# Another table of due-time shifts in a list-scheduled attention and MLP kernel on one core

## The chip, the core and the metric

The kernel runs on one core of a Trainium2 chip. The core has a matrix engine (TensorE, PE, with its weight loads PEld), a vector engine (VectorE, DVE), a scalar engine (ScalarE, ACT), a general engine (GpSimd, POOL) and a queue engine (SyncE, SP) that issues nearly all transfers. The metric is device time in microseconds for one execution; less is better. Instructions of one engine run in the order in which the program issued them; engines wait for one another through semaphores. So an order that is planned ahead is the order that the chip must follow.

## What is computed

Four batches of four heads, 1088 tokens, head size 32. Each token is projected twice to eight numbers (S1 and S2); the outer product of both is its feature vector of 64. Linear attention is made of these features, and its result, 4352 tokens of 128, goes through a two-layer MLP with a leaky relu whose slope is given per hidden unit.

```
def phi(x):
    a = np.einsum('rd,bhsd->bhsr', S1, x)
    b = np.einsum('rd,bhsd->bhsr', S2, x)
    return np.einsum('bhsi,bhsj->bhsij', a, b).reshape(*x.shape[:-1], r * r)
q_p, k_p = (phi(q), phi(k))
kv = np.einsum('bhsf,bhsd->bhfd', k_p, v)
z = np.sum(k_p, axis=2)
num = np.einsum('bhsf,bhfd->bhsd', q_p, kv)
den = np.einsum('bhsf,bhf->bhs', q_p, z)[..., None] + 1e-06
...
h = x @ w_in
g = np.maximum(h, 0.0) + alpha * np.minimum(h, 0.0)
return (g @ w_out)
```

## The kernel before

The kernel is written as a list of 762 operations, each with an engine (or several to choose from), a duration for each, what it depends on and which buffers it holds. A planner (`plan`, from line 168) puts them in order at build time, and the kernel then emits them in that order.

**What the operations are.** For each batch b, the keys side makes features in two halves: `kb.0T` and `kb.1T` transpose, `...ab` projects (L636), `...abc` copies out of PSUM, `...kp` multiplies (L653). Batch 0 transposes on PE (L626), the others on DVE (L681). The last 64 tokens of each batch are the rest: `kr0.0`, `kr0.1` and `kr1`. `z0.0`, `z0.1`, `zr0` (L719, L733) and `kv0.0`, `kv0.1`, `kvr0` (L706, L726) accumulate the sums over tokens. `zm`, `finz`, `zc` (L751, L757, L763 and 764) bring the sum z into the form that the denominator needs; `kvc`, `fin`, `kvW` (L361, L766, L361) do this for the numerator.

The queries side: `qT` transposes on DVE (L855 for batch 0, which is cut into the halves `q0.0` and `q0.1`; L815 otherwise), `a` and `b` project on PE (L872 or L828), `ac0`, `ac1` copy and `mul0`, `mul1` multiply (L884 or L842). Then `ratio`: `den` and `num` on PE (L785), `dT` transposes the denominator (L792), `rc` takes the reciprocal (L798, L799), `rr` spreads it by a transpose (L801), and `x0`, `x1` multiply it with the numerator (L807). `x0` of `q0.0` is what the first MLP matmul waits for.

The MLP works in ten chunks g of tokens: seven of 512 and three of 256. Each has 16 matmuls `hg.c` (L955), each with a relu `rg.c` on ACT (L961) or DVE (L963), 16 matmuls `og.c` (L976; L973 in the last chunk) that add to one PSUM bank, and one more, `Wg`, with the product W of both weights, for the leaky part. `oTg` transposes the sum (L983) and `stg` stores it by SP. All o-matmuls of all chunks but the last share PSUM bank 7, so `o1.0` can't start before `oT0` has read it. Eight buffers hold relu results and at most four PSUM banks hold h.

The weights are prepared on the way, in four parts each: `w_in_bf` casts w_in (ACT or DVE, L361), `w_a` scales w_out for the o-matmuls (ACT at L573, or DVE or POOL at L556), `w_b` scales it for W (ACT or POOL), `w_hi` and `w_lo` split w_b in two bf16 parts, `winT` and `winTc` transpose w_in, `Wmm` (L598) and `W` (L604, L605) make W.

**What sets the order.** The planner takes due times from the MLP, which is given 10.2 us per chunk of 512 from 14.5 us on, and passes them backward: an operation is due 1.6 times the duration (plus latency and 70 ns) ahead of the earliest that needs it. To each due time it adds the entry of a table `SHIFT`, in ns. Then it steps through the list: among the first 120 operations still waiting by due time, those whose inputs are planned are candidates; on each engine the one that is due first wins among those that can start within 120 to 300 ns of the earliest, and over the engines the one that starts first is placed. An operation that may go to two engines is put where it ends first. Where PE would idle between 4 and 20 us, fill matmuls (L499) are put in. So the table changes order and, for operations with a choice, the engine, and also the number of fills; instructions and data stay as they are. Loads have names that begin with `ld` and due times near -1,000,000; no entry of the table names one.

```
for o in ops:
    o.due += SHIFT.get(o.name, 0)
waiting = sorted(ops, key=lambda o: o.due)
```

Inherited due times (before the shift), in ns, of the operations that matter later: kr0.0T 1,370; q0.0b 3,342; zr0 3,661; zm0 4,317; kvr0 8,021; kvc0 8,693; q0.0rc 9,179; fin0 9,239; q0.1T 11,556; w_in_bf 12,147 (first part); w_b0 to w_b3 15,763; w_a1 15,873; w_lo0 to w_lo3 17,873; w_a3 20,783; W0 23,445.

Of the kernel before, what the change touches and what calls it, by code (L numbers as in the profile page):

```python
# [34 lines left out]
class Op:  # L35
# [30 lines left out]
    "S": 6140, "W": -7785, "W0": 1995, "W1": -3593, "W2": 5, "W3": -3870, "W4": -6766, "W5": 16353,  # L66
    "W6": -376, "W7": 10186, "W8": -1052, "W9": -1646, "Wmm": -6987, "alpha": -2765, "alphaT": -56356,
    "fin0": 14889, "fin1": -96, "fin2": 6846, "fin3": 4117, "finz0": 414, "finz1": -2297, "finz2": 14064,
    "finz3": 14913, "h0.0": -48890, "h0.1": -44482, "h0.10": -20550, "h0.11": -20506, "h0.12": -20265,
    "h0.13": -19045, "h0.14": -18399, "h0.15": -12121, "h0.2": -42632, "h0.3": -37456, "h0.4": -25806,  # L70
    "h0.5": -22156, "h0.6": -21957, "h0.7": -22369, "h0.8": -22128, "h0.9": -21948, "h1.0": -6078,
    "h1.1": -6568, "h1.10": -4424, "h1.11": -3438, "h1.12": -3826, "h1.13": -2710, "h1.14": -896,
    "h1.15": -1170, "h1.2": -5552, "h1.3": -4703, "h1.4": -4984, "h1.5": -3823, "h1.6": -4399, "h1.7": -4190,
    "h1.8": -3910, "h1.9": -4410, "h2.0": -635, "h2.1": 32, "h2.10": 137, "h2.11": -311, "h2.12": -365,
    "h2.13": -528, "h2.14": -850, "h2.15": -1064, "h2.2": -533, "h2.3": -1016, "h2.4": -1486, "h2.5": -1619,
    "h2.6": -824, "h2.7": -937, "h2.8": -591, "h2.9": -530, "h3.0": -2018, "h3.1": -920, "h3.10": -705,
    "h3.11": -966, "h3.12": -493, "h3.13": -526, "h3.15": 55, "h3.2": -1159, "h3.3": -730, "h3.4": -1309,
    "h3.5": -1793, "h3.6": -2054, "h3.7": -2660, "h3.8": -2424, "h3.9": -1487, "h4.0": -1546, "h4.1": -2165,
    "h4.10": -2919, "h4.11": 400, "h4.13": 89, "h4.14": -69, "h4.15": -83, "h4.2": -876, "h4.3": -488,
    "h4.4": -976, "h4.5": -1517, "h4.6": -2066, "h4.7": -2461, "h4.8": -2353, "h4.9": -2894, "h5.0": -1154,  # L80
    "h5.1": -1149, "h5.10": -295, "h5.11": -640, "h5.12": -1074, "h5.13": -1192, "h5.14": 291, "h5.15": 217,
    "h5.2": -1589, "h5.3": -1771, "h5.4": -1691, "h5.5": -1874, "h5.6": -1510, "h5.7": -1214, "h5.8": 88,
    "h5.9": -205, "h6.0": -207, "h6.1": 288, "h6.10": -1799, "h6.11": -2260, "h6.12": -2137, "h6.13": -1884,
    "h6.14": -207, "h6.15": -104, "h6.2": -207, "h6.3": -360, "h6.4": -101, "h6.5": -327, "h6.6": -529,
    "h6.7": -810, "h6.8": -1438, "h6.9": -2068, "h7.0": -975, "h7.1": -920, "h7.10": -1394, "h7.11": -993,
    "h7.12": -885, "h7.13": -667, "h7.14": 74, "h7.15": 22, "h7.2": -1209, "h7.3": -1250, "h7.4": -1497,
    "h7.5": -1686, "h7.6": -1144, "h7.7": -1096, "h7.8": -1336, "h7.9": -1256, "h9.0": -56, "h9.1": 634,
    "h9.10": 1533, "h9.11": 1394, "h9.12": 3304, "h9.13": 4471, "h9.14": 8625, "h9.15": 30374, "h9.2": 1277,
    "h9.3": 1488, "h9.4": 1818, "h9.5": 2075, "h9.6": 1949, "h9.7": 1698, "h9.8": 1822, "h9.9": 1642,
    "ident": -5301, "identb": 4245, "k0.0T": -338245, "k0.0Tc": -222654, "k0.0ab": -204581,  # L90
    "k0.0abc": -148771, "k0.0kp0": -2818, "k0.0kp1": -2947, "k0.1T": -290955, "k0.1Tc": -106980,
    "k0.1ab": -55631, "k0.1abc": -158, "k0.1kp0": -2312, "k0.1kp1": -1676, "k1.0T": -7361, "k1.0ab": -5266,
    "k1.0abc": -4605, "k1.0kp": 499, "k1.1T": -6359, "k1.1ab": -6458, "k1.1abc": -5045, "k1.1kp": -4738,
    "k2.0T": -28437, "k2.0ab": -4092, "k2.0abc": -1298, "k2.0kp": 2242, "k2.1T": 2146, "k2.1ab": 2146,
    "k2.1abc": 5610, "k2.1kp": 6306, "k3.0T": -25545, "k3.0ab": -24652, "k3.0abc": -23865, "k3.0kp": 1001,
    "k3.1T": 149, "k3.1ab": -1456, "k3.1abc": 580, "k3.1kp": 1938, "kr0.0T": -46499, "kr0.0Tc": -14777,
    "kr0.0ab": -12941, "kr0.0abc": -1149, "kr0.1T": -4092, "kr0.1Tc": -3579, "kr0.1ab": -3528,
    "kr0.1abc": -3313, "kr1T": -16436, "kr1Tc": -9432, "kr1ab": -1384, "kr1abc": 9835, "kv0.0": -2625,
    "kv0.1": 1851, "kv1": -996, "kv2": 4392, "kv3": 818, "kvW1": -5462, "kvW2": 7589, "kvW3": 17434,
    "kvc0": 5255, "kvc1": 78, "kvc2": 7320, "kvr0": 2609, "kvr1": 2446, "kvr2": 8823, "kvr3": 11490,  # L100
    "mask4": -1518, "masks": -28026, "o0.0": -12138, "o0.1": -1771, "o0.10": -3699, "o0.11": 89, "o0.12": 42,
    "o0.13": 5930, "o0.14": 98, "o0.15": -3161, "o0.2": -320, "o0.3": -3922, "o0.4": -4360, "o0.5": -3046,
    "o0.6": -82, "o0.7": -13490, "o0.8": -7352, "o0.9": -5660, "o1.0": -53, "o1.1": 8059, "o1.10": 14816,
    "o1.11": 22404, "o1.12": 449, "o1.13": 4844, "o1.14": 17486, "o1.15": 7036, "o1.2": 6355, "o1.3": -71,
    "o1.4": -32, "o1.5": 8264, "o1.6": 11885, "o1.7": 9436, "o1.8": 21020, "o1.9": 15581, "o2.0": 3602,
    "o2.1": 25261, "o2.10": 14347, "o2.11": 6322, "o2.12": 174, "o2.13": -321, "o2.14": 1774, "o2.15": 2276,
    "o2.2": 21551, "o2.3": 10241, "o2.4": 13814, "o2.5": 21013, "o2.6": -90, "o2.7": 11854, "o2.8": 108,
    "o2.9": 935, "o3.0": 2349, "o3.1": 20927, "o3.10": 8081, "o3.11": 5347, "o3.12": 608, "o3.13": 11675,
    "o3.14": 1466, "o3.2": 8241, "o3.3": 12758, "o3.4": 22143, "o3.5": 5685, "o3.6": 3532, "o3.7": 481,
    "o3.8": 4495, "o3.9": 23059, "o4.1": 497, "o4.10": 8949, "o4.11": 8, "o4.13": 4363, "o4.14": -225,  # L110
    "o4.15": 121, "o4.2": 1775, "o4.3": 2282, "o4.4": 1603, "o4.5": -1726, "o4.6": -78, "o4.7": 24007,
    "o4.8": 617, "o4.9": 1000, "o5.0": 4551, "o5.1": 22714, "o5.10": 18207, "o5.11": -425, "o5.12": 2511,
    "o5.13": -144, "o5.14": 9197, "o5.15": 5612, "o5.2": 13081, "o5.3": 15045, "o5.4": 17002, "o5.5": 2911,
    "o5.6": 10540, "o5.7": 8104, "o5.8": -342, "o5.9": -144, "o6.0": -25, "o6.1": 6809, "o6.10": 2075,
    "o6.11": 1537, "o6.12": 19356, "o6.13": -1218, "o6.14": 223, "o6.15": 16936, "o6.2": 15551, "o6.3": 1979,
    "o6.4": 986, "o6.5": 2904, "o6.6": 11826, "o6.7": 20308, "o6.8": 7660, "o6.9": 8842, "o7.0": 260,
    "o7.1": 211, "o7.10": 29630, "o7.11": 4680, "o7.12": 10219, "o7.13": 711, "o7.14": 25929, "o7.15": 27443,
    "o7.2": 2632, "o7.3": 268, "o7.4": 5360, "o7.5": -423, "o7.6": 19131, "o7.7": 14612, "o7.8": 3,
    "o7.9": 52263, "o8.0": 1783, "o8.1": 22008, "o8.10": 27673, "o8.11": 23944, "o8.12": 4252,
    "o8.13": 126570, "o8.14": 37728, "o8.15": 3387, "o8.2": 3039, "o8.3": 51554, "o8.4": 16336, "o8.5": 6119,  # L120
    "o8.6": 379, "o8.7": 18531, "o8.8": 42466, "o8.9": 1979, "o9.0": 2274, "o9.1": 10388, "o9.10": 49229,
    "o9.11": 22575, "o9.12": 56832, "o9.13": 49904, "o9.14": 30415, "o9.15": 66470, "o9.2": 61690,
    "o9.3": 52093, "o9.4": 17752, "o9.5": 24707, "o9.6": 38495, "o9.7": 76119, "o9.8": 27064, "o9.9": 46410,
    "oT0": -12790, "oT1": -408, "oT2": -3211, "oT3": 4518, "oT4": 616, "oT5": -3024, "oT6": -7579,
    "oT7": -1161, "oT8": -2287, "oT9.0": -536, "oT9.1": -449, "q0.0T": -219038, "q0.0a": -202701,
# [942 lines left out]
```

## Time and profile before

| | us |
|---|---|
| median of 5 runs | 113.79 |
| lowest and highest of them | 111.95, 114.03 |
| profiled execution, its own time | 112.38 |
| its span, first to last instruction | 110.6 |
| PE busy in it | 105.3 |
| DVE busy | 83.2 |
| ACT busy | 75.9 |
| POOL busy | 24.1 |

The profile is of one execution. A row of the timeline gives start, duration, engine, source line, operation, output and inputs with shapes, the count, and in brackets how long the engine had idled before and what released it. In the chain of waits each piece is what the next had to wait for, followed back from the end; "issue" is time in which nothing visible was waited for. Matmuls overlap: one of 512 columns is listed with 0.38 us, but the next starts 0.215 us after it, so PE's busy time says that work was there, not how dense it was. The granted clock is given in tenths of full speed.

### The profile page before, as it was taken

To read this page: it belongs to the slowest core of one execution; us is meant where nothing else is said; L and a number is where in the kernel's file an instruction comes from. 1 tells how busy PE (TensorE), PEld (TensorE's weight loads), DVE (VectorE), ACT (ScalarE), POOL (GpSimd) and SP (SyncE) were. 2 spreads that over 40 slices of the span, in tenths; PEclk is the share of its full clock that TensorE was granted. 3 is DMA by queue.
4 is the path that set the end of the run, shared out by engine and by line. 5 is a ranking of instruction groups with operands and counts; after the bars stand their busy time and mean duration, and the time that the engine had idled before them with its cause. 6 is when DMAs were issued, how large, how long until landed. Compare 5 with 4: busy or idle time off the path is not lost.

```text
span 110.6 us, 3534 instructions
## 1 busy us (share of the span) xinstructions
PE 105.3 (95%) x1458; PEld 54.5 (49%) x1458; DVE 83.2 (75%) x156; ACT 75.9 (69%) x162; POOL 24.1 (22%) x24
## 2 busy tenths in 40 slices
PE   7999988989999999999999999999999999999980
PEld 2577333534454663447443353444534544588870
DVE  3188869898998488996667978986548798669840
ACT  2454599998489681891983963597596278787880
POOL 2040089990029108921500000000000000000000
PEclk9999999999999999999999999999999999999999
DMA  2999999779589640041002200050040005033222
GB/s 59 264 300 286 306 277 335 134 247 297 79 272 280 99 79 0 6 71 30 0 0 47 48 6 0 6 92 3 0 81 14 6 0 95 0 56 57 33 49 59
DMA packets 37536, 11.25 MB, mean 102 GB/s; under 512 B 27008, under 2 KB 37520, under 8 KB 37520
## 3 DMA queue, kind: packets, MB, share of 16 engines
q1 hardware_dynamic: 37264, 10.95, 42.9%
q8 instruction: 11, 0.18, 0.7%
q10 hardware_dynamic: 256, 0.08, 0.3%
q14 instruction: 5, 0.04, 0.1%
HBM read 8.80 MB, written 2.23 MB: 100 GB/s over the span
## 4 chain that ended last, share of the span: by engine, by line
PE 75%; DMA 8%; SPq 7%; POOL 5%; issue 2%; ACT 0%; DVE 0%; DVEq 0%
PE ps L976 26%; PE ps L955 24%; DMA w_out_f<-in_moe_w_out_dram 8%; SPq L385 7%; PE ps L785 7%; PE ps L828 6%; PE ps L636 3%; PE ps L706 3%; POOL w_b_f L556 2%; POOL w_a_bf L556 2%; PE ps L973 2%; PE ps L598 2%; POOL w_hl L556 1%; PE ps L757 1%; PE ps L726 1%
## 5 line engine op out<-in xcount | busy, mean ns | idle before, releaser
L955 PEld LDWEIGHTS <-w_in_bf 128*128 128x128 bf16 x160 | 15.0, 97 | 15.4 <-issue 3.6
L955 PE MATMUL ps<-xT__96,w_in_bf 128*128 128x512 bf16 (+1 forms) x80 | 21.5, 358 | 0.4 <-ACT rh__82 L961 0.4
L976 PEld LDWEIGHTS <-w_a_bf 128*128 128x128 bf16 x144 | 13.6, 97 | 14.4 <-issue 2.0
L955 PE MATMUL ps<-xT__97,w_in_bf 128*128 128x512 bf16 (+1 forms) x80 | 19.2, 336 | 0.0
L961 ACT ACTIVATE rh__82<-ps 128x512 bf16<-128x512 f32 (+1 forms) x23 | 12.6, 548 | 4.9 <-PE ps L955 4.6
L961 ACT ACTIVATE rh__83<-ps 128x512 bf16<-128x512 f32 (+1 forms) x22 | 11.9, 542 | 3.6 <-PE ps L955 3.6
L961 ACT ACTIVATE rh__84<-ps 128x512 bf16<-128x512 f32 (+1 forms) x16 | 8.5, 531 | 0.9 <-PE ps L955 0.6
L961 ACT ACTIVATE rh__86<-ps 128x512 bf16<-128x512 f32 (+1 forms) x14 | 7.9, 562 | 1.0 <-PE ps L976 0.5
L792 DVE STREAM_TRANSPOSE dt__78<-ps 128x1024 f32<-128x1024 f32 (+2 forms) x6 | 5.6, 937 | 3.6 <-PE ps L785 3.6
L976 PE MATMUL ps<-rh__83,w_a_bf 128*128 128x512 bf16 (+1 forms) x22 | 7.9, 359 | 0.0
L961 ACT ACTIVATE rh__87<-ps 128x512 bf16<-128x512 f32 (+1 forms) x12 | 6.2, 518 | 2.0 <-PE ps L955 1.8
L961 ACT ACTIVATE rh__85<-ps 128x512 bf16<-128x512 f32 x11 | 6.6, 604 | 0.9 <-PE ps L955 0.9
L976 PE MATMUL ps<-rh__82,w_a_bf 128*128 128x512 bf16 (+1 forms) x20 | 7.3, 363 | 0.0
L976 PE MATMUL ps<-rh__84,w_a_bf 128*128 128x512 bf16 (+1 forms) x19 | 6.8, 357 | 0.3 <-POOL w_a_bf L556 0.3
L976 PE MATMUL ps<-rh__86,w_a_bf 128*128 128x512 bf16 (+1 forms) x20 | 7.1, 353 | 0.0
L976 PE MATMUL ps<-rh__85,w_a_bf 128*128 128x512 bf16 (+1 forms) x19 | 6.8, 356 | 0.0
L828 PE MATMUL ps<-qT__74,Sab 32*64 32x512 f32 x96 | 6.7, 613 | 0.0
L983 DVE STREAM_TRANSPOSE oT__91<-ps 128x512 f32<-128x512 f32 (+1 forms) x8 | 5.4, 680 | 1.6 <-PE ps L976 1.5
L963 DVE TENSOR_SCALAR rh__85<-ps 128x256 bf16<-128x256 f32 (+1 forms) x10 | 5.3, 527 | 1.7 <-PE ps L955 1.0
L963 DVE TENSOR_SCALAR rh__86<-ps 128x512 bf16<-128x512 f32 (+1 forms) x8 | 4.4, 552 | 2.5 <-PE ps L955 1.0
L976 PE MATMUL ps<-rh__87,w_a_bf 128*128 128x512 bf16 (+1 forms) x17 | 6.0, 355 | 0.0
L653 POOL TENSOR_TENSOR kp__70<-ab__68 128x1024 f32<-128x1024 f32 x2 | 3.9, 1956 | 9.5 <-ACT ab__68 L361 4.8
(157 smaller groups left out, 216.4 us busy)
## 6 DMA issues: line engine op xcount, KB each, us to landing
out_dram<-oT__91 SPq DMA_DIRECT2D x28, 64.0 KB, 1.9
k<-in_k_dram SPq DMA_DIRECT2D x3, 512.0 KB, 4.1
q<-in_q_dram SPq DMA_DIRECT2D x3, 512.0 KB
v<-in_v_dram SPq DMA_DIRECT2D x12, 128.0 KB, 5.4
w_in_f<-in_moe_w_in_dram SPq DMA_DIRECT2D x2, 512.0 KB, 7.0
w_out_f<-in_moe_w_out_dram SPq DMA_DIRECT2D x2, 512.0 KB, 7.9
k<-in_k_dram SPq DMA_DIRECT2D x2, 256.0 KB, 3.2
q<-in_q_dram SPq DMA_DIRECT2D x2, 256.0 KB
```

The source lines that it names most:

```text
L385: (nc.sync if eng == "sp" else nc.scalar).dma_start(dst, src)
L556: return lambda e: (nc.vector if e == "dve" else nc.gpsimd).tensor_tensor(out=out, in0=a, in1=b, op=what)
L636: nc.tensor.matmul(ps(bf)[lo + i:lo + i + aw, j * 64:(j + 1) * 64], sb(bT)[:, j * cnt + i:j * cnt + i + aw], S12blk.rearrange("p h c -> p ...
L653: (nc.vector if e == "dve" else nc.gpsimd).tensor_tensor(out=dst, in0=i0, in1=i1, op=ALU.mult)
L785: nc.tensor.matmul(dst, w, mv, start=True, stop=True, skip_group_check=True)
L792: nc.vector.transpose(bview(sb(dt), [[1, nn]]).rearrange("p (c n) -> p c n", c=2), ps(bd)[:, :, :ncp])
L828: nc.tensor.matmul(ps(bufs[t // 2])[64 * c:64 * c + 64, t % 2, :nf], bview(Sab[32 * t:32 * t + 32, i], [[1, R]]), moving(sb(bq), t, c), st ...
L955: nc.tensor.matmul(ps(b)[:, :n], w_in_bf[:, c * 128:(c + 1) * 128], xs(), start=True, stop=True)
L961: nc.scalar.activation(sb(br)[:, :n], ps(b)[:, :n], ACTF.Relu)
L963: nc.vector.tensor_scalar_max(sb(br)[:, :n], ps(b)[:, :n], 0.0)
L976: nc.tensor.matmul(ps(bo)[:, :n], w, y(), start=c == 0, stop=c == NC)
L983: o = op("dve", dv(n) + 40, lambda e: nc.vector.transpose(bview(sb(boT), [[1, n]]), ps(bo)[:, :n]), [last], [bo, boT], 80, end, f"oT{g}")
```

## The change

The whole change is another table `SHIFT`, with 699 entries in place of 675. All else, `plan` among it, is the same. The diff, cut to entries that the text below speaks of and some of their neighbours:

```
 SHIFT = {
...
-    "S": 6140, "W": -7785, "W0": 1995, "W1": -3593, "W2": 5, "W3": -3870, "W4": -6766, "W5": 16353,
+    "S": -7836, "Sab": -21631, "W": -9717, "W0": 13130, "W1": -2261, "W2": 158, "W3": -5573, "W4": -762,
...
-    "fin0": 14889, "fin1": -96, "fin2": 6846, "fin3": 4117, "finz0": 414, "finz1": -2297, "finz2": 14064,
+    "alphaT": -113674, "fin0": -197, "fin1": 1558, "fin2": 5231, "fin3": 10679, "finz0": -6860, "finz1": 259,
...
-    "k3.1T": 149, "k3.1ab": -1456, "k3.1abc": 580, "k3.1kp": 1938, "kr0.0T": -46499, "kr0.0Tc": -14777,
+    "k3.1abc": 1165, "k3.1kp": 1931, "kr0.0T": -61323, "kr0.0Tc": -47226, "kr0.0ab": -29513, "kr0.0abc": 2222,
...
-    "kv0.1": 1851, "kv1": -996, "kv2": 4392, "kv3": 818, "kvW1": -5462, "kvW2": 7589, "kvW3": 17434,
-    "kvc0": 5255, "kvc1": 78, "kvc2": 7320, "kvr0": 2609, "kvr1": 2446, "kvr2": 8823, "kvr3": 11490,
+    "kvW3": 13555, "kvc0": -17087, "kvc2": 1986, "kvc3": 1108, "kvr0": -12312, "kvr1": 2269, "kvr2": 7638,
...
-    "q0.0ac0": -192252, "q0.0ac1": 14918, "q0.0b": -4711, "q0.0dT": -153737, "q0.0den": -156593,
-    "q0.0mul1": -3827, "q0.0num": -101573, "q0.0rc": 1638, "q0.0rr": -126171, "q0.0x0": -47987, "q0.1T": 1102,
+    "q0.0T": -240062, "q0.0a": -215260, "q0.0ac0": -192157,
+    "q0.0ac1": -8807, "q0.0b": 685, "q0.0dT": -181547, "q0.0den": -190132, "q0.0mul0": -3079,
+    "q0.0mul1": 10478, "q0.0num": -89181, "q0.0rc": -14012, "q0.0rr": -163676, "q0.0x0": -80815,
+    "q0.1T": 2090,
...
-    "w_a1": 933, "w_a2": 9447, "w_a3": -1769, "w_b0": -3090, "w_b1": 20475, "w_b2": -17819, "w_b3": -1940,
+    "st9.1": 68233, "w_a0": 3313, "w_a1": 10350, "w_a2": 10033, "w_a3": 9313, "w_b0": -5006, "w_b1": 539,
+    "w_b2": -7570, "w_b3": -9465,
...
-    "w_in_bf": 1696, "w_lo0": 3902,
+    "w_in_bf": 4483,
+    "w_lo0": 15386,
...
-    "zm0": -9912,
+    "zm0": -44722, "zr0": -22838,
 }
```

zr0 has no entry before. The lines of the diff are cut here to the entries in question, so some are shorter than in the source.

## Prediction

> **What bounds the kernel now.** I read the page first, then the chain of waits in order of time, then busy time by windows, then the timeline. The page says what is full:
>
> ```profile
> PE 105.3 (95%) x1458; PEld 54.5 (49%) x1458; DVE 83.2 (75%) x156; ACT 75.9 (69%) x162; POOL 24.1 (22%) x24
> PEclk9999999999999999999999999999999999999999
> PE 75%; DMA 8%; SPq 7%; POOL 5%; issue 2%; ACT 0%; DVE 0%; DVEq 0%
> ```
>
> PE is busy for 95% of the span at full granted clock, and three quarters of the chain are PE. The chain in order of time says when it is something else:
>
> ```profile
> 9.00 8.43 DMA w_out_f<-in_moe_w_out_dram
> ...
> 17.50 2.04 POOL w_b_f L556 x2
> ...
> 22.78 1.01 POOL w_a_bf L556
> ...
> 23.83 0.82 PE ps L976 x3
> ...
> 51.17 0.30 DVE fs__99 L751
> 51.49 0.28 ACT fs__100 L361
> ```
>
> Until 23.83 the end hangs on the second half of w_out and on POOL's preparation of it. From there to 107.5 the chain is PE but for one gap of about 0.6 us at 51. Then 3.1 us of last copy and store follow. Busy time by windows (length, then PE, PEld, DVE, ACT and POOL with their instructions, clock, DMA) shows which engines are full while the pipeline fills:
>
> ```profile
> 12.00:16.00 4.00, 3.71 (x62) 1.46 (x55) 2.63 (x6) 2.65 (x8) 1.79 (x2) 1.00 1.11 275
> 16.00:20.00 4.00, 3.58 (x29) 1.26 (x28) 3.68 (x6) 3.97 (x8) 3.86 (x5) 1.00 1.16 322
> 20.00:24.00 4.00, 3.66 (x29) 1.99 (x28) 3.99 (x6) 4.00 (x9) 4.00 (x5) 1.00 0.63 154
> ```
>
> Between 16 and 24 ACT, DVE and POOL are full and PE is not; between 12 and 16 ACT and DVE idle a third of the time, because h0.0 has not started. The timeline shows the chain of the first reciprocal, and two lines that I need later:
>
> ```profile
> 6.98 1.12 PE L872 MATMUL ps<-qT__74,Sab 32*64 32x256 f32 x32
> 8.03 0.27 PE L626 MATMUL ps<-ident,kr 64*128 64x64 f32 x1
> 8.62 0.22 ACT L361 COPY kT__64<-ps 128x64 f32<-128x64 f32 x1
> 8.76 1.30 DVE L884 TENSOR_TENSOR aq__76<-ps,aq__76 128x512 f32<-128x512 f32 x2
> 11.37 0.70 DVE L855 STREAM_TRANSPOSE qT__74<-q 128x512 f32<-128x512 f32 x1
> 11.52 0.66 PE L785 MATMUL ps<-aq__76,zc 64*32 64x256 f32 x16
> 12.29 0.72 DVE L792 STREAM_TRANSPOSE dt__78<-ps 128x512 f32<-128x512 f32 x1 [0.21 <-PE ps L785]
> 14.84 0.69 DVE L807 TENSOR_TENSOR xT__96<-ps,rr__80 128x512 bf16<-128x512 f32 x1 [0.58 <-PE ps L785]
> ...
> 22.73 1.05 POOL L556 TENSOR_TENSOR w_a_bf<-w_out_f,omaT 128x512 bf16<-128x512 f32 x1
> ...
> 33.06 0.38 PE L976 MATMUL ps<-xT__96,W_bf 128*128 128x512 bf16 x1
> ```
>
> The denominator (L785) starts at 11.52 though its products (L884) end at 10.06: it waits for z, which waits for the k rest (8.03, 8.62). x0 (L807) then idles 0.58 us for the numerator.
>
> **The change, part by part.** The table alone changes, so work per engine is the same, but for operations that may go to one of two engines. A due time is the inherited one, which the backward pass of the source gives, plus the shift, in the planner's ns. I compare these sums, old to new, and do not know the order that comes of them.
>
> *First chain.* The k-rest transpose falls from -45,129 to -59,953, zr0 from 3,661 to -19,177, zm0 from -5,595 to -40,405, and the reciprocal from 10,817 to -4,833; q0.0b rises from -1,369 to 4,027. So the k rest may pass the second half of L872 on PE (0.56 us) and the copies on ACT (8.62 less the 8.30 at which its transpose ended, 0.32): z comes up to 0.88 earlier. But q0.0b, its copies and products come later, by the 0.27 of L626 and the zm (0.28) that is put between. Bounds: a gain of 11.52 - 10.06 = 1.46, if nothing but the products gates; a loss of 0.6, if q0.0b waits for all of kv0.0 (L706 at 9.01, 0.64 long; then 0.56 on PE, 1.2 on ACT, 0.65 on DVE: 12.1). I take a gain of 0.5, nearest to 0.88 less 0.27 and part of the zm.
>
> *Prefetches put behind.* q0.1T (12,658 to 13,646) passes behind the reciprocal. It costs nothing now: it runs at 11.37 to 12.07, and the transpose at 12.29 waits on PE. If it goes later, q0.1a (14.73) has 2.6 us of slack. The w_in casts (13,843 to 16,630) lie on ACT at 11.37, with 3.3 us to h0.0. Both: 0.
>
> *Numerator.* kvr0, kvc0 and fin0 fall by 15 to 22 thousand. The 0.58 that x0 idles can go; four fill matmuls on PE (12.28 to 13.31) and a 0.66 gap inside the numerator stand in the way, and I see neither in the table. Bounds 0 to 0.58; I take 0, since those two rows hold it.
>
> *Preparation of w_out.* w_b1 falls from 36,238 to 16,302, w_a1 rises from 16,806 to 26,223, w_a3 from 19,014 to 30,096, w_lo0 from 21,775 to 33,259. POOL does ten such steps of 1.04 to 1.15 without a break but one of 0.2 between 14.21 and 24.77. With w_b1 first, w_a3 (22.73) may end one step later: -0.34 (the wait of PE on it gone) to +1.04. I take 0: behind it stand a numerator (0.66) and q1a (1.11) ready for PE, 1.77 of cover; without them it costs the 1.04. On SBUF ports: POOL's steps keep 1.04 whatever DVE does, and DVE took one of them (0.69) only after POOL had finished. The Trainium skill (SBUF — State Buffer, Who interferes with whom) says that a DVE instruction with two SBUF inputs and a GpSimd one that reads SBUF lock each other out, which would speak against sending w_a or w_lo to DVE meanwhile. By that rule the sum would be worse by an estimated 1.0; no row here shows it.
>
> *After 24 us.* PE's work is the same 83 us, so only waits count: the 0.62 at 51 may go, others may come. x1.0, the second of batch 0, ends at 27.56 and is used at 28.19: new waits are possible, bounded by the rival below. I take 0.
>
> *Queues and fills.* No load has a shift, so SP's loads keep their order; stores move, and SP is free 0.5 us before its last issue (107.80), so 0 to +0.5 at the end, taken 0. Fills before h0.0 (seven from 8.50 to 12.93) may change in number: each is 0.22, on PE that then has no other work. The granted clock is full in every slice. The Trainium skill (TensorE: Matmul & The Clock Gate, The HAM clock gate) says an idle window of about 3.4 us halves the clock; by it an order with too few fills would cost an estimated 1.7 (one such window at half speed). The longest PE gap here is under 1 us.
>
> *Sum.* -0.5 against the profiled execution: 112.38 us, of which 110.6 are span and 1.8 lie around it: 111.9. The median of the runs, 113.79, stands 1.41 above that execution; the same term on it gives **113.3 us**. The 0.5 lasts to the end only if ACT and DVE use it (they idle 1.35 us each between 12 and 16); POOL's data do not come earlier for it.
>
> **Rivals.** About 2%, 2.3 us, is what a measurement of this kernel tells from no change.
>
> A. The start gives all: 1.46, plus 0.42 (PE's wait for the relu at 17.02), 0.34 (for w_a at 23.83) and 0.62 (at 51): 2.84, so 111.0. For: each wait is in the profile. Against: w_a hangs on data that landed at 17.43, which the table does not move, and for the whole 1.46 the numerator would have to end 2.0 us sooner (1.46 and the 0.58 that x0 waits for it).
>
> B. Nothing: the prefetch never stood in the way (q0.1T ran in a wait on PE), and the end hangs on w_out's landing and POOL's work: 113.8. The change then does not do what it says.
>
> C. POOL's reorder costs its 1.04 with cover gone, less 0.5: 114.3.
>
> D. Slower: W0, the last matmul of chunk 0, at 33.06, goes from due 25,440 to 36,575, 11.1 us. All o-matmuls share one PSUM bank, so o1.0 waits for W0 and its transpose. PE can go on with h1 until eight relu buffers are full (8 x 0.215 = 1.7 us), then only with attention; the pieces of it from 36.80 to 44.46 add up to 6.6 us. If W0 really is 11.1 later, 11.1 - 8.3 = 2.8 stay; less 0.5, 2.3: 116.1. It decides from 8.3 us of delay on, or earlier if that attention work is not ready, for which DVE, full to 3.99 of 4 between 20 and 24, speaks. Against: PE takes what is ready, due or not, and little else is.
>
> **How the numbers follow.** Forecast 0.38 (its own range 112.4 to 114.2), A 0.16, B 0.16, C 0.08, D 0.22. Faster is A, 0.16. Within 2% are the forecast, B and 0.06 of C (the rest of C is with two such steps late, 115.4 and a wait more): 0.60. Slower are D and that rest: 0.24. The range, 111.0 to 116.4, goes from A's price to a little past D's (0.3, the cover that may be smaller) and leaves out about half of A and of D, 0.19.
>
> **What would show it.** First chain: the first reciprocal (13.26) about 0.5 earlier and h0.0 (15.78) too; the k rest at L626 before the second half of L872. Preparation: w_b steps before w_a on POOL, and PE's wait for w_a_bf near 23.8. D: the W_bf matmul of chunk 0 well after 33, and PE idle between 24 and 45. It is wrong if the granted clock falls below 9 anywhere, if PE between 24 and 107 shows waits of over 1 us, or if relus change engine so that ACT or DVE becomes full in the long stage.

## Result, and the profile after

| | before | after |
|---|---|---|
| median of all runs made side by side, us | 113.18 (42 runs, 111.86 to 114.22) | 113.64 (23 runs, 113.07 to 117.22) |
| ratio of the times, 95% interval | | 1.0079 [1.0054, 1.0104] |
| profiled execution, its own time | 112.38 | 113.67 |
| its span | 110.6 | 111.9 |

By the ratio the change costs 0.8%, some 0.9 us. The medians of all executions lie only 0.46 us apart (0.4%): those of before spread over 2.4 us, and 18 of its 42 are shorter than the shortest of after. So the sign is sure, the size is 0.4 to 0.8%, and the forecast (0.5 us less) had the other sign. (Some disturbed executions are left out of all ratios; the profiles of e2, e3, e5, e10 and e15 below are of such executions, 0.9 to 2.4 us above their kernels' medians in the first four, so they show places and not prices.)

The page of after, engines and chain: PE is busy for 0.9 us more than before.

```profile
PE 106.2 (95%) x1461; PEld 55.1 (49%) x1461; DVE 83.6 (75%) x157; ACT 74.8 (67%) x160; POOL 25.2 (23%) x25
PEclk9999999999999999999999999999999999999999
...
PE 92%; ACT 2%; DVE 1%; issue 1%
PE ps L958 27%; PE ps L979 27%; PE ps L788 8%; PE ps L831 6%; PE ps L502 5%; PE ps L709 4%; PE ps L639 4%; PE ps L629 2%; PE ps L875 2%; PE ps L976 2%; PE ps L601 2%; PE ps L760 1%; ACT rh__82 L964 1%; PE ps L729 1%; PE ps L592 1%
```

The chain of waits has gone from 75% PE to 92%. POOL and w_out have left it, and L502, matmuls that work on nothing, has come in with 5%: 3.14 us are seven warm-up matmuls at the very start, 2.45 us the fills. (Lines of after lie 3 below those of before: fills L499 become L502, the numerator L785 becomes L788, L872 becomes L875, L955 becomes L958.) The chain of after, in order of time:

```profile
10.85 0.25 PE ps L729 x8
11.10 0.43 PE ps L760 x2
...
12.29 0.22 PE ps L502
12.51 1.02 PE ps L788 x32
13.53 0.64 issue
14.17 1.91 PE ps L502 x8
16.07 1.07 PE ps L875 x32
```

And the timeline of after, PE first, then x0 on DVE:

```profile
12.44 0.66 PE L788 MATMUL ps<-aq__76,zc 64*32 64x256 f32 x16
12.89 0.64 PE L788 MATMUL ps<-aq__76,kvW 64*32 64x256 f32 x16
14.17 1.91 PE L502 MATMUL ps<-const-bfloat16-1.0 128*128 128x512 bf16 x8 [0.64 <-issue]
16.00 1.12 PE L875 MATMUL ps<-qT__74,Sab 32*64 32x256 f32 x32
17.06 0.39 PE L958 MATMUL ps<-xT__96,w_in_bf 128*128 128x512 bf16 x1
...
15.31 0.69 DVE L810 TENSOR_TENSOR xT__96<-ps,rr__80 128x512 bf16<-128x512 f32 x1
```

The numerator now stands right behind the denominator, and x0 (15.31) no longer idles for it: the 0.58 is gone. But x0 ends at 16.00, and h0.0 starts at 17.06. Between them PE runs the first projection of the second query half (L875), which the eight fills have held up to 16.00. Before, the same projection began at 14.73, and h0.0 0.25 us after x0's end:

```profile
13.24 0.65 PE L785 MATMUL ps<-aq__76,kvW 64*32 64x256 f32 x12
14.18 0.62 PE L785 MATMUL ps<-aq__76,kvW 64*32 64x256 f32 x4 [0.29 <-issue]
14.73 1.12 PE L872 MATMUL ps<-qT__74,Sab 32*64 32x256 f32 x32
...
15.78 0.39 PE L955 MATMUL ps<-xT__96,w_in_bf 128*128 128x512 bf16 x1
```

The same two executions cut at six points, and with them all kernels of the study but e15, which is e12 again, from the timelines (times in us). "kv" is the first projection of the keys (L636 of before), "den" the first denominator, W2 the last matmul of chunk 2.

| kernel | kv starts | kv to den | den to x0's end | x0's end to h0.0 | h0.0 to W2 | W2 to last matmul |
|---|---|---|---|---|---|---|
| before | 5.63 | 5.89 | 4.01 | 0.25 | 42.04 | 49.46 |
| before, another execution (e4) | 5.65 | 6.33 | 4.75 | 0.25 | 42.12 | 49.46 |
| e3 before, its fills moved | 5.71 | 6.58 | 4.00 | 2.05 | 41.78 | 49.47 |
| e7 before, no num fills | 5.51 | 5.87 | 3.54 | 0.14 | 42.93 | 49.47 |
| e13 before, hold | 5.99 | 5.74 | 4.61 | 0.19 | 42.59 | 49.47 |
| e14 before, no num fills, hold | 6.01 | 5.79 | 3.54 | 0.05 | 42.23 | 49.46 |
| e10 before to 30 us, then after | 6.53 | 7.26 | 4.18 | 0.05 | 41.51 | 50.01 |
| after | 6.19 | 6.24 | 3.57 | 1.05 | 41.42 | 50.07 |
| e1 after, short fills | 6.01 | 6.43 | 4.38 | 0.05 | 41.25 | 50.07 |
| e2 after, no fills | 5.51 | 6.83 | 3.53 | 0.05 | 43.72 | 50.07 |
| e9 after to 30 us, then before | 6.40 | 7.64 | 4.17 | 0.05 | 41.28 | 49.56 |
| e11 the same, no fills | 5.67 | 6.46 | 3.53 | 0.05 | 41.38 | 49.54 |
| e12 the same, hold | 5.59 | 6.77 | 3.54 | 0.05 | 41.52 | 49.55 |
| e5 new table for the start alone | 5.66 | 6.30 | 3.61 | 4.06 | 41.71 | 49.74 |
| e6 the same, no fills | 6.29 | 7.85 | 3.53 | 0.05 | 41.66 | 49.73 |
| e8 the same, hold | 5.53 | 6.35 | 3.53 | 0.05 | 42.42 | 49.73 |

From before to after the six columns give +0.56, +0.35, -0.44, +0.80, -0.62 and +0.61, together, but for rounding, the 1.27 by which the last matmul is later (107.28 to 108.55). The first of them is no part of the change: kv starts from 5.51 to 6.53 with the old order of the start and from 5.51 to 6.40 with the new one. Two executions of before (e4 is the same kernel) already differ by 1.3 us in span, 110.6 and 111.9, so one profile against another says where, and the ratios say how much.

### The profile page after: what moved, and what is told of

It is laid out like the page before. It is cut to its first block, busy times and chain, and to the rows that moved or that the text cites. A ratio compares the mean times of both kernels' runs of the same rounds, so it can differ in the third digit from the quotient of the medians.

```text
span 111.9 us, 3533 instructions
## 1 busy us (share of the span) xinstructions
PE 106.2 (95%) x1461; PEld 55.1 (49%) x1461; DVE 83.6 (75%) x157; ACT 74.8 (67%) x160; POOL 25.2 (23%) x25
## 4 chain that ended last, share of the span: by engine, by line
PE 92%; ACT 2%; DVE 1%; issue 1%
PE ps L958 27%; PE ps L979 27%; PE ps L788 8%; PE ps L831 6%; PE ps L502 5%; PE ps L709 4%; PE ps L639 4%; PE ps L629 2%; PE ps L875 2%; PE ps L976 2%; PE ps L601 2%; PE ps L760 1%; ACT rh__82 L964 1%; PE ps L729 1%; PE ps L592 1%
## 5 line engine op out<-in xcount | busy, mean ns | idle before, releaser
L958 PEld LDWEIGHTS <-w_in_bf 128*128 128x128 bf16 x160 | 15.0, 97 | 15.8 <-issue 4.1
L958 PE MATMUL ps<-xT__96,w_in_bf 128*128 128x512 bf16 (+1 forms) x80 | 21.9, 358 | 0.4 <-ACT rh__82 L964 0.4
L958 PE MATMUL ps<-xT__97,w_in_bf 128*128 128x512 bf16 (+1 forms) x80 | 20.0, 336 | 0.0
L964 ACT ACTIVATE rh__82<-ps 128x512 bf16<-128x512 f32 (+1 forms) x21 | 11.6, 551 | 7.8 <-PE ps L958 7.7
L964 ACT ACTIVATE rh__83<-ps 128x512 bf16<-128x512 f32 (+1 forms) x19 | 10.4, 545 | 3.0 <-PE ps L958 2.9
L964 ACT ACTIVATE rh__85<-ps 128x512 bf16<-128x512 f32 (+1 forms) x18 | 9.7, 541 | 2.2 <-PE ps L979 1.4
L979 PE MATMUL ps<-rh__82,w_a_bf 128*128 128x512 bf16 (+1 forms) x22 | 7.9, 360 | 0.0
L964 ACT ACTIVATE rh__86<-ps 128x512 bf16<-128x512 f32 (+1 forms) x14 | 7.4, 529 | 0.3 <-PE ps L958 0.2
L964 ACT ACTIVATE rh__84<-ps 128x512 bf16<-128x512 f32 (+1 forms) x14 | 7.3, 520 | 0.4 <-PE ps L958 0.2
L979 PE MATMUL ps<-rh__83,w_a_bf 128*128 128x512 bf16 (+1 forms) x21 | 7.4, 354 | 0.0
L964 ACT ACTIVATE rh__87<-ps 128x512 bf16<-128x512 f32 (+1 forms) x12 | 6.6, 547 | 0.9 <-PE ps L958 0.5
L502 PE MATMUL ps<-const-bfloat16-1.0 128*128 128x512 bf16 x17 | 5.8, 481 | 1.4 <-PEq L1055 0.8
L979 PE MATMUL ps<-rh__85,w_a_bf 128*128 128x512 bf16 (+1 forms) x20 | 7.0, 352 | 0.0
L364 ACT COPY aq__76<-ps 128x512 f32<-128x512 f32 (+2 forms) x6 | 3.8, 658 | 4.3 <-PE ps L875 2.5
L966 DVE TENSOR_SCALAR rh__88<-ps 128x512 bf16<-128x512 f32 (+1 forms) x11 | 6.1, 555 | 0.5 <-PE ps L958 0.4
L979 PE MATMUL ps<-rh__84,w_a_bf 128*128 128x512 bf16 (+1 forms) x18 | 6.5, 361 | 0.0
L979 PE MATMUL ps<-rh__86,w_a_bf 128*128 128x512 bf16 (+1 forms) x18 | 6.4, 356 | 0.0
L656 POOL TENSOR_TENSOR kp__70<-ab__67 128x512 f32<-128x512 f32 (+1 forms) x2 | 3.0, 1510 | 13.6 <-PE ps L639 7.9
```

Of the source, the lines that this page charges most:

```text
L364: nc.scalar.copy(dst, src)
L502: nc.tensor.matmul(PS[:, 7], ones(128), ones(512), start=True, stop=True, skip_group_check=True)
L958: nc.tensor.matmul(ps(b)[:, :n], w_in_bf[:, c * 128:(c + 1) * 128], xs(), start=True, stop=True)
L964: nc.scalar.activation(sb(br)[:, :n], ps(b)[:, :n], ACTF.Relu)
L966: nc.vector.tensor_scalar_max(sb(br)[:, :n], ps(b)[:, :n], 0.0)
L979: nc.tensor.matmul(ps(bo)[:, :n], w, y(), start=c == 0, stop=c == NC)
```

## Experiments

Theory 1: the eight fills ahead of q0.1a run late and are the loss. Rivals: the new order of the chain itself; the order far behind the start. All ratios are against the kernel before, run beside each on the same chip.

**e1, after with the eight fills cut to 32 columns** (the count of instructions is kept; only fills, which nobody reads, are smaller):

```
-        dummy(o.fill)
+        dummy(o.fill, 32 if o.name == "q0.1a" else 512)
```

> Kernel after, with the eight fill matmuls ahead of the first half of the q0.1 projection cut from 512 to 32 columns; their number stays. Theory F (the changed kernel starts its MLP late because eight fills of 0.22 us follow a stall of PE that ends at 14.17 us, and h0.0 is queued behind them): the projection starts at about 14.5 instead of 16.00, h0.0 at about 16.1 instead of 17.06, and the time falls by 0.5 to 1.0 us against the kernel after, to that of the kernel before or below. Rival R (the 0.57 us that the changed kernel's profile is late at 6.2 us is chance of that execution, and the lasting cost is in the later order): h0.0 falls too, but the time stays within 0.2 of the kernel after, ratio to before 1.006 to 1.010.

Measured: 1.0019 [0.9983, 1.0056], after being at 1.0079. The timeline of e1:

```profile
13.63 0.35 PE L502 MATMUL ps<-const-bfloat16-1.0 128*128 128x32 bf16 x8
13.91 1.17 PE L875 MATMUL ps<-qT__74,Sab 32*64 32x256 f32 x32
16.88 0.81 PE L958 MATMUL ps<-xT__96,w_in_bf 128*128 128x512 bf16 x3 [1.80 <-DVE xT__96 L810]
...
13.97 1.03 DVE L801 TENSOR_SCALAR dt__78<-dt__78 128x16 f32<-128x16 f32 x1
...
13.92 1.04 POOL L559 TENSOR_TENSOR w_b_f<-w_out_f,alphaT 128x512 f32<-128x512 f32 x1 [4.62 <-DMA w_out_f<-in_moe_w_out_dram]
```

L875 starts at 13.91, and PE then idles 1.80 us for x0: with short fills the projection is no longer what h0.0 waits for. In this execution the chain is longer for another reason: the small addition (L801, 16 elements in each partition) takes 1.03 where it took 0.22 in after, and it ends as POOL's first scaling of w_out does (13.92 + 1.04).

**e2, after without the eight fills** (only fills left out):

```
-        dummy(o.fill)
+        dummy(0 if o.name == "q0.1a" else o.fill)
```

> Kernel after without those eight fills at all, so PE's instruction count falls by sixteen as well. Theory F: as with short fills, and if the stall at 13.53 to 14.17 belongs to an instruction count it falls later in the program, into the projection or among the first h-matmuls; time 0.5 to 1.0 us below the kernel after. Rival R: within 0.2 of the kernel after.

Measured: 0.9973 [0.9931, 1.0016]. Against after that is 1.06%, or 1.2 us, more than the 0.80 of the profile's column; the intervals allow 0.4%. The stall of 0.64 us is still there, after as many matmuls as in after, and now holds the projection itself (it ends 1.28 us after the block of instructions that is told of under e4 has landed, at 12.80):

```profile
14.08 1.12 PE L875 MATMUL ps<-qT__74,Sab 32*64 32x256 f32 x32 [0.64 <-DVE dt__78 L801]
```

**e3, before with its four num fills put behind the numerator, as eight ahead of q0.1a** (nothing left out):

```
-        dummy(o.fill)
+        dummy(8 if o.name == "q0.1a" else 0 if o.name == "q0.0num" else o.fill)
```

> Kernel before, with the four fills ahead of the numerator moved behind it and four more added there, so that eight stand ahead of the q0.1 projection, as in the kernel after. Theory F: the projection starts about 1.2 us later than 14.73 and h0.0 about 1.2 later than 15.78; the time rises by 0.4 to 0.9 us, to that of the kernel after. Rival R: the time stays within 0.2 us of the kernel before.

Measured: 1.0054 [1.0009, 1.0100]. By the ratio the fills of after, put into before, make it slower; by the medians of all executions on that chip (113.66 and 113.56) hardly, so this run supports theory 1 only weakly. The timeline of e3:

```profile
13.92 0.67 PE L785 MATMUL ps<-aq__76,kvW 64*32 64x256 f32 x16 [0.71 <-DVE dt__78 L792]
15.45 1.91 PE L499 MATMUL ps<-const-bfloat16-1.0 128*128 128x512 bf16 x8 [0.86 <-issue]
```

**e4, before once more** (no edit, one execution).

> Kernel before once more, for a second profile of it. Rival R and theory F alike hold the difference at the first k projection (5.62 in the profile of before, 6.19 in that of after, from the same instructions in the same order) for chance: then this profile, and those of the other three, show starts spread between about 5.6 and 6.2, whichever table they have. If all kernels with the new table start at 6.2 and all with the old one at 5.6, the table causes it.

Measured: 113.67 us, span 111.9. Its timeline beside the first execution's:

```profile
13.70 0.65 PE L785 MATMUL ps<-aq__76,kvW 64*32 64x256 f32 x12
15.37 0.62 PE L785 MATMUL ps<-aq__76,kvW 64*32 64x256 f32 x4 [1.02 <-issue]
15.93 1.12 PE L872 MATMUL ps<-qT__74,Sab 32*64 32x256 f32 x32
...
13.50 0.81 DVE L798 TENSOR_SCALAR dt__78<-dt__78 128x16 f32<-128x16 f32 x1
16.03 0.69 DVE L807 TENSOR_TENSOR xT__96<-ps,rr__80 128x512 bf16<-128x512 f32 x1 [0.69 <-PE ps L785]
```

The gap inside the numerator that the prediction saw (0.66 from start to start there, 0.29 of it idle) is 1.02 of idleness here, in the same place, after 12 of 16 matmuls, and named "issue": PE waits for nothing that the program asked for. In the DMA view the one transfer of instructions (queue q8, 16 KB) of this stretch lands at 14.01 in e4, and PE goes on at 15.37; 12.82 and 14.18 in before; 12.82 and 14.17 in after; 13.98 and 15.45 in e3; 14.00 and 15.34 in e5. So PE is out of instructions near its 440th until 1.34 to 1.47 us after the block has landed. Where it landed at 12.17 (e1), there was no gap.

The planner knows of this wait. It counts PE's instructions in blocks of 256, from 62 on (`BLOCK`, `BEFORE`), and holds PE until the next block is there, which it puts at 14.66 us with either table. Fills are what it puts into a wait. `plan` is plain Python and gives its order without the chip: with before's table it has the whole numerator and its four fills ahead of that wait, with after's table the numerator at 12.28 and then eight fills until q0.1a at 14.66. But it expects the wait after the 450th matmul or weight load, and the rows have it after 441 (before) and 439 (after). So in before it falls inside the numerator, and in after ahead of the very fills that were to cover it: meant for 12.73 to 14.66, they ran from 14.17 to 15.92, when x0 was nearly there.

Theory 2: which part of the table carries the start?

**e5, before's table with only the 50 entries of the first stage taken from the new one** (nothing left out):

```
+SHIFT.update({'masks': 10220, 'kvc0': -17087, 'kvW0': 1827, 'S': -7836, ...
+for _k in ['ident']:
+    SHIFT.pop(_k)
```

> The table of before with only the entries of the first stage from the new table (batch 0 keys, their rest, z and kv of batch 0, the first q0.0 chain, masks and the setup): 50 entries. The planned PE order is then that of after up to 20 us (planned) and that of before from 12 us on, so the new start stands alone, its eight fills with it. Theory S (two costs: the fills in the start, 0.7 to 1.2 us as measured by taking them away, and a later order that loses 0.5 to 0.6 us of PE after 58 us): time 0.4 to 0.6 us below the kernel after, ratio to before 1.001 to 1.005; from the W-matmul of chunk 2 to PE's end 49.46 us as in before, not 50.07. Rival (the later order costs nothing, the start all): as the kernel after, 1.006 to 1.010.

Measured: 1.0069 [1.0027, 1.0111]. The timeline of e5 and its busy time by windows (length, PE, PEld, DVE, ACT, POOL, granted clock, DMA):

```profile
15.34 3.31 PE L503 MATMUL ps<-const-bfloat16-1.0 128*128 128x512 bf16 x8 [2.29 <-issue]
18.58 0.44 PE L876 MATMUL ps<-qT__74,Sab 32*64 32x256 f32 x3
```

```profile
15.30:18.50 3.20, 3.16 (x8) 0.99 (x7) 0.27 (x1) 0.00 (x0) 1.77 (x3) 0.54 1.14 335
```

Here PE stood still for 2.29 us, the granted clock fell to 0.54, and the eight fills took 3.31 us. (That execution took 116.2 us, the median of e5 is 113.81.) The loss of the start is there with the start's entries alone.

**e6, e5 without the eight fills** (only fills left out; the edit of e2 on e5).

> The same with the eight fills ahead of the q0.1 projection left out. Theory S: 0.7 to 1.2 us below the run with them, so ratio to before 0.991 to 0.997: the new order of the first chain is a gain once its fills are gone, since the numerator then ends ahead of PE's stall at its instruction 440. Rival (fills and new start cancel): 0.998 to 1.003.

Measured: 1.0056 [1.0014, 1.0099], hardly better than e5, unlike e2 against after. So in e5 and e6 something else holds the time. These two prepare w_out in before's order, which the table shows to be slower after an early start (below); that this is what holds them is argued, not shown.

**e7, before without its four num fills** (only fills left out):

```
-        dummy(o.fill)
+        dummy(0 if o.name in ('q0.0num',) else o.fill)
```

> Kernel before without the four fills ahead of the first numerator (12.28 to 13.31). If fills are the cost and not the order, the numerator starts at about 12.85, is done before PE's stall, and the old order gains as much as the new one: ratio 0.993 to 0.997. If the new order matters by itself (numerator right behind the denominator), this stays at 0.998 to 1.002, as the numerator waits for kvW at 12.75 and the stall is met in the projection instead.

Measured: 0.9989 [0.9957, 1.0020]. In its profile h0.0 is 0.72 earlier than in before (15.06), but h0.0 to W2 takes 42.93 in place of 42.04: the earlier start is lost again by 58 us.

**e8, e6 with POOL held until the first reciprocal is written** (w_b0, POOL's first scaling of w_out, is emitted right behind q0.0rc, and ahead of it a scratch copy that reads the reciprocal; fills left out):

```
+    order[k:k] = late
...
+            nc.gpsimd.tensor_copy(hold, tiles["dt"][rc.bufs[0].slot][:, 0, 1:2])
```

> The new start without its eight fills, and POOL's first scaling of w_out held until the first reciprocal is written (one more copy of 128 numbers on POOL that reads it). Theory P (the small DVE addition ahead of the reciprocal took 0.18 us in three profiles and 0.64, 0.81 and 1.03 in three others, each time until POOL's scaling ended, because w_out had landed earlier than planned): the addition takes 0.18 to 0.22 in this profile, with POOL starting after the reciprocal; the time falls by 0.1 to 0.5 us against the run without the hold, in its upper half most. Rival (POOL's chain is the limit until 24 us): the hold delays POOL by up to 1 us and the time rises by 0 to 0.5 us.

Measured: 1.0018 [0.9982, 1.0054], 0.4% below e6, with intervals that overlap. The addition took 0.18.

Theory 3: the loss at the start and a loss after 58 us are two things. The order of one kernel up to 30 us was joined to that of the other for all that follows; the planner's choice was replaced by a written list, `ORDER`, of operations and engines from the two plans, buffers chosen by its own rule.

**e9, after to 30 us, then before** (nothing left out):

```
-        for o in waiting[:WINDOW]:
+        for o in waiting[:1]:
```

> The planned order of the changed kernel on every engine up to 30 us, and the planned order of the kernel before for all that is left; nothing is left out. Theory (the loss is two losses: eight fill matmuls that run late at the start, and 0.60 us in the order after 58 us, of which the profile showed 50.07 against 49.46 from the last matmul of chunk 2 to the last matmul): the later loss goes, 49.46 again, and the time is that of the changed kernel less 0.6, a ratio near 1.003. Rival (the start alone is the loss, and the later 0.6 is given back by waits that were there before): about 1.008, as the changed kernel.

Measured: 1.0056 [1.0019, 1.0092]; W2 to the last matmul 49.56.

**e10, before to 30 us, then after** (the same edit, the other list).

> The other half: the planned order of the kernel before up to 30 us, and that of the changed kernel for the rest; nothing is left out. Theory: the start is that of the kernel before, and from the last matmul of chunk 2 to the last matmul it takes 50.07, as in the changed kernel: 0.6 us, a ratio near 1.005. Rival (the later order costs nothing of itself): 49.5 and a ratio of 1.000.

Measured: 1.0049 [1.0016, 1.0082]; W2 to the last matmul 50.01. That agrees with a price of the later order of its own; how sure it is, is said below.

**e11, e9 without the eight fills** (only fills left out; the edit of e2).

> As the kernel with the new order up to 30 us, and also without the eight fill matmuls ahead of the first projection of the second query half; only fills, whose results nobody reads, are left out. Theory: both losses gone, and what is left is what the new order of the start is worth: the changed kernel without fills had 0.997, less 0.6 us makes 0.992, so about 112.3 where the kernel before has 113.2. Rival (the start is worth nothing, and 0.997 was chance): 1.000.

Measured: 0.9972 [0.9932, 1.0012], against 1.0056 of e9 on the same chip: the fills cost 0.84%, or 0.95 us, and the two intervals do not meet. (The profile of e9 does not show it: there x0 ends at 18.21, later than the fills and q0.1a, and h0.0 follows it by 0.05.) The 0.992 that was expected did not come.

**e12, e11 with POOL held** (the edit of e8).

> As the one before it, and POOL's first scaling of w_out is held until the first reciprocal is written, by a copy of one column that reads it, so that the two cannot lock each other out; a scratch copy is added, only fills are left out. Theory (POOL's step and the small addition ahead of the reciprocal lock each other out in executions in which the first half of w_out lands early, 0.1 to 0.9 us): the addition at 0.18 in every execution, and 0.3 to 0.5 us less than without the hold, 0.988 to 0.990. Rival (POOL's step is needed at once): as without it, or up to 0.5 us worse, since POOL then is late with w_a.

Measured: 0.9957 [0.9921, 0.9992], the only version whose interval lies below 1. The timeline of e12:

```profile
13.88 0.18 DVE L913 TENSOR_SCALAR dt__78<-dt__78 128x16 f32<-128x16 f32 x1
14.09 0.26 DVE L914 RECIPROCAL dt__78<-dt__78 128x16 f32<-128x16 f32 x1
...
14.41 0.19 POOL L1161 COPY hold<-dt__78 128x1 f32<-128x1 f32 x1 [5.54 <-DVE dt__78 L914]
14.55 1.04 POOL L671 TENSOR_TENSOR w_b_f<-w_out_f,alphaT 128x512 f32<-128x512 f32 x1
```

One question is left: is that gain the new order's, or only the fills' and the hold's?

**e13, before with the hold** (a scratch copy added):

> The kernel before with POOL's first scaling of w_out held until the first reciprocal is written; a scratch copy is added, nothing is left out. If the lock between POOL's step and the small addition costs 0.1 to 0.9 us in executions in which w_out lands early: 0.997 to 0.999. If POOL's work is what the later start hangs on: 1.000 to 1.004.

Measured: 1.0019 [0.9979, 1.0060]: nothing gained. In its profile x0 waits 1.18 us for the numerator anyway, and the numerator for kvW (see "Prefetches" below).

**e14, before with the hold and without its num fills** (only fills left out):

> The same without the four fills ahead of the numerator, which are all that is left out. If the gain of the version with the new start came from the fills and the hold alone, this one has the same ratio as that one, 0.995 to 0.997. If the new order of the start is worth something of itself (the numerator right behind the denominator, before the stall of PE), this one is 0.3 to 0.5 us behind it: 0.999 to 1.000.

Measured: 0.9982 [0.9937, 1.0028].

**e15, e12 once more.**

> The new order up to 30 us, without the eight fills and with the hold, once more beside the two others on the same chip: 0.994 to 0.998 if its first ratio was no chance; 1.000 if it was.

Measured: 0.9963 [0.9909, 1.0017]. That agrees with e12, but does not tell it from e14: whether the new order of the start is worth something beyond its fills is open, and the best estimate, 0.9963 against 0.9982, is 0.2%. Nor is it a safe gain: the median of all 12 executions was 113.71 (e14: 112.74), where before had 113.38, and five of the twelve had a mean clock of 0.968 to 0.985. The profiled one shows what happened to it. Its timeline, and a window:

```profile
12.94 0.64 PE L900 MATMUL ps<-aq__76,kvW 64*32 64x256 f32 x16
15.60 1.68 PE L987 MATMUL ps<-qT__74,Sab 32*64 32x256 f32 x32 [2.02 <-DVE rr__80 L916]
```

```profile
16.00:20.00 4.00, 3.78 (x38) 1.41 (x24) 2.43 (x5) 2.77 (x6) 4.00 (x5) 0.57 1.19 319
```

The block of instructions landed at 14.10, PE stood still from 13.58 to 15.60, and from 16 to 20 us the mean clock was 0.57. (The releaser that the row names, DVE's transpose of the reciprocal, is none of this projection's inputs; in e11 the projection ran at 13.15, ahead of it.)

## Why the prediction was wrong, step by step

**Queues and fills: a step that failed, and the costliest.** It let the fills "change in number: each is 0.22, on PE that then has no other work", and took 0. Their number went from seven to ten, but their place decided. Four stood ahead of the numerator, where they cost something only if it was late; eight now stand ahead of q0.1a, and behind them, in the order of PE, q0.1a and h0.0. PE had other work by the time they ran, 1.44 us behind their plan: the numerator ended at 13.53 in place of 12.73, and the stall at "issue" added 0.64. Price: 0.80 in the profile, 0.95 by e9 against e11. Taking them away shows it (e1, e2, e11); adding them to before (e3) agrees, weakly.

**After 24 us: taken as 0, and it is +0.6.** In each profile with the later order of the new table, W2 to the last matmul takes 50.01 to 50.07, and with before's 49.46 to 49.56 (49.73 in e5, e6 and e8, left open at the end). Between the profiles of before and after it is no single wait: +0.10 in chunk 3, +0.14 in chunk 6, +0.31 in chunk 8. The last one, in the chain of after:

```profile
104.44 0.12 PE ps L979
104.56 0.13 issue
104.70 0.44 DVE rh__89 L966
105.14 0.04 issue
```

PE waits there for one relu on DVE. The prediction's threshold of a wait over 1 us was too coarse: waits of 0.1 to 0.3 add up to 0.55. By timing the price is less sure: e10 shows 0.5% where e9 against after, and e11 against e2, show 0.2 and 0.0, on different chips.

**First chain: -0.5 forecast, +0.35 to +0.57 came.** This is the other step that failed, and the one that gave the forecast its sign, as the only term not taken as 0. From kv to the denominator before needs 5.89 and after 6.24; all kernels with before's start need 5.74 to 7.26 (median 5.89), those with the new one 6.24 to 7.85 (median 6.46). The k rest did not pass the second half of L872. What passed is the rest of kv: L729 (0.25) now stands ahead of finz (L760) on PE, where it stood behind it, and a fill (0.22) stands right ahead of the denominator; both are in the chain of after shown above, 0.47 together. (Before had two fills there, which ended before z was ready.) The first reciprocal went from 13.26 to 14.21 in place of 0.5 earlier. The plan had said as much: it has the denominator at 11.72 with the old table and at 11.83 with the new one, and h0.0 at 15.71 with both.

**Numerator: 0 forecast, -0.4 came.** The row of fills and the gap that "stand in the way" were read as fixed, but the table moved the numerator ahead of both. From den to x0's end the chain alone is 3.53 to 3.54. Before needs 4.01, with a longer stall 4.75 (e4), with a late kvW 4.61 (e13), and 3.54 in e7 and e14, without its fills. (The 4.00 of e3 is the lock told under "SBUF ports".) The upper bound, 0.58, was nearer than the value taken.

**Prefetches: 0 forecast, and the execution that was read hid their cost.** The prediction held the two w_in casts on ACT against h0.0. But on ACT the copy kvW, which the numerator needs, stands right behind them, and they wait for w_in. In before they were done as the numerator's input came:

```profile
11.37 1.14 ACT L361 CAST w_in_bf<-w_in_f 128x512 bf16<-128x512 f32 x2
12.48 0.27 ACT L361 COPY kvW<-ps 128x128 f32<-128x128 f32 x1
```

In e13, with the same order on ACT, w_in landed later, and the numerator waited for it:

```profile
13.53 1.14 ACT L361 CAST w_in_bf<-w_in_f 128x512 bf16<-128x512 f32 x2 [1.93 <-DMA w_in_f<-in_moe_w_in_dram]
14.57 0.26 ACT L361 COPY kvW<-ps 128x128 f32<-128x128 f32 x1
...
14.88 0.67 PE L785 MATMUL ps<-aq__76,kvW 64*32 64x256 f32 x16 [1.35 <-ACT kvW L361]
```

In e7 and e14 kvW is late too (13.10 and 13.07), within the time that x0 has. In after the copy (12.33) is ahead of the casts (12.49). So the table does put a prefetch behind work that is waited for; that is worth about 1.1 us in an execution like e13 and nothing in the two of before. The other prefetch, q0.1T, still runs (12.08) ahead of the transpose at 13.21.

**Preparation of w_out: 0 forecast, -0.6 came.** POOL's order in after:

```profile
13.10 1.04 POOL L559 TENSOR_TENSOR w_b_f<-w_out_f,alphaT 128x512 f32<-128x512 f32 x1 [3.62 <-DMA w_out_f<-in_moe_w_out_dram]
14.09 2.04 POOL L559 TENSOR_TENSOR w_a_bf<-w_out_f,omaT 128x512 bf16<-128x512 f32 x2
...
19.35 2.04 POOL L559 TENSOR_TENSOR w_a_bf<-w_out_f,omaT 128x512 bf16<-128x512 f32 x2
```

w_b1 went to ACT, so w_a is complete at 21.4 in place of 23.8, and PE's wait for it has gone. That wait is 0.34 in before (h0.0 at 15.78), and with before's preparation and an earlier h0.0 0.39 (e8, 15.47), 0.52 (e14, 15.38) and 0.61 (e7, 15.06); e13 has 0.56, its first half of w_out having landed later (POOL starts on it at 15.18). No kernel with after's preparation has it. The window of after that answers to one shown of before:

```profile
20.00:24.00 4.00, 4.00 (x45) 2.09 (x44) 3.72 (x6) 4.00 (x8) 3.44 (x4) 1.00 0.56 131
```

PE is full there (4.00, before 3.66). From h0.0 to W2 the kernels with after's preparation need 41.25 to 41.52 (but for e2, whose clock falls to 0.74 at 16 to 20). Those with before's need 42.04 to 42.93 where h0.0 starts before 17 us (15.06: 42.93, 15.38: 42.23), and 41.51 to 41.78 only where it starts at 17.7 or later. So the sentence that "POOL's data do not come earlier" for an earlier h0.0 held, and explains e7: with before's preparation an earlier start is not passed on.

**SBUF ports.** The Trainium skill (SBUF — State Buffer, Who interferes with whom) was weighed for two inputs on DVE, and no row then showed it. The runs show the lock elsewhere: the addition ahead of the reciprocal, one input, takes 0.18 when POOL is idle or begins later, and 0.64 (e3), 0.81 (e4), 0.82 (e9), 0.83 (e10) and 1.03 (e1) when one of POOL's scalings of w_out has begun before it. It then ends within 0.05 of POOL's step, as it does with 0.22 (after) and 0.26 (e5), where that step was nearly over. With POOL held (e8, e12, e13, e14, e15) it takes 0.18 each time. The same section lists such scalar additions among those that can take the shared ports, and says that whoever issues first keeps them for the whole instruction; the rows agree. That the trace of before did not show it was chance: there w_out landed after the reciprocal.

**Clock.** In the profiled execution of after the clock is full in every slice, as forecast, but three of its 23 executions (116.35 to 117.22 us) had a mean clock of 0.983 to 0.985. The Trainium skill (TensorE: Matmul & The Clock Gate, The HAM clock gate) names an idle window of about 3.4 us. In e5 a standstill of 2.29 us and in e15 one of 2.02 went with a loss of the clock, in e1 one of 1.80 did not, and in e2 no gap ahead of the loss was longer than 1.19. Windows of e2 (length, PE, PEld, DVE, ACT, POOL, granted clock, DMA):

```profile
14.48:17.90 3.42, 1.53 (x34) 0.65 (x19) 3.07 (x5) 2.94 (x9) 2.70 (x3) 1.00 0.98 280
17.90:21.32 3.42, 3.40 (x9) 1.13 (x8) 2.04 (x4) 2.40 (x5) 3.37 (x5) 0.50 1.00 296
```

The clock is at a half for one stretch of 3.42 us; in e5 (14.83 to 18.25) and e15 (16.03 to 19.44) it is the same, and PE was busy for 1.40 and 1.39 of the 3.42 us before. So no idle window of 3.4 us was needed here; a stretch with PE busy for less than half of it was enough, though not always: e1, with 1.53 busy from 13.46 to 16.88, kept its clock. The longest gap of PE in the trace of before was under 1 us, and the next execution of the same kernel (e4) had 1.02.

**Rivals.** A did not come: its start was to give 1.46 and lost. D did not: W0 is at 33.76, 16.7 after h0.0 (17.3 before). C did not: POOL's new order was a gain. B's reason, that the prefetch never stood in the way, holds for the execution that it was read from and not for e13; its sum does not hold, since the order brought gains and losses of 0.4 to 0.8 that nearly cancel. No rival had the fills. That the time lies inside the range is luck: the mechanisms named for a slower kernel, C and D, did not come.

## What to carry to other kernels

An instruction put in to fill an idle gap is free only while the gap is where the plan has it: look at what stands behind it on its engine, and ask what happens if it runs 1.4 us late. When a planned order changes everywhere, cut both traces at the same few points and compare stretch by stretch; here stretches of +0.8 to -0.6 hid in a net of 0.8%, and forecasting 0 for four of them was wrong four times. Where a planner makes the order at build time, run it with both tables before forecasting: the place of the fills, the later denominator and kvW ahead of the casts all stand in its output. Take a second execution of the same kernel before one profile is compared with another: the start alone moved by 1.2 us.

## What the hardware showed that was not expected

- PE ran out of instructions in its first 15 us: a gap, mostly named "issue", of 0.3 to 2.3 us near its 440th instruction, ended 1.3 to 1.7 us after a block of 16 KB of instructions had landed, while the loads kept the DMA engines full (share 1.11 from 12 to 16 us in after). The Trainium skill (Runtime: NRT & Kernel Launch, Instruction fetch mechanics) calls the crossing of a 16 KiB boundary mostly hidden; here it was not.
- An addition of 128 x 16 elements took 0.18 us with POOL idle and 1.03 where POOL had begun a step 0.05 us before it.
- After 2.29 us of standstill the next eight matmuls of 512 columns took 3.31 us in place of 1.91 (e5). A mean clock under 0.99 is on record for 2 of 127 executions of before that were run beside the experiments, for 9 of 60 with eight fills ahead of q0.1a (after, e3, e5, e9), and for 19 of 96 with the eight or the four fills left out (e2, e6, e7, e8, e11, e12, e14, e15). So the fills of before seem to keep the clock up, and those of after stand behind the stall; no run was made to show this alone.
- Left open: e5, e6 and e8 have before's planned order of PE behind about 26 us, and still need 0.27 more from W2 to the last matmul (49.73), all of it between chunks 6 and 7, where a relu on ACT starts 0.28 later. No run shows why.
